# Second layer: the sums of weight blocks on VectorE, ten tiles transposed once and kept in DRAM by columns

## The chip, the core and the metric

The kernel runs on 1 core of a Trainium2 chip. The metric is the device time of one execution in microseconds (us), and a kernel's time is the median of its runs. A core has TensorE (PE in the profile; its weight loads are listed apart as PEld), VectorE (DVE), ScalarE (ACT), GpSimd (POOL) and SyncE (SP), which here only issues transfers. Each engine works through a queue of its own in order, and a wait at the head of a queue holds what is behind it.

## The reference, cut to what matters

Attention over pooled keys gives x, 2304 rows of 512. A first layer sends each row to one of eight experts. The second layer, which the change touches, sends every row through all eight:

```python
def _moe2_ref(x, w_gate, w1, w2):          # x 2304x512, w1 8x512x1024, w2 8x1024x512
    logits = x @ w_gate
    P = np.exp(logits - logits.max())
    for _ in range(8):
        P /= P.sum(1, keepdims=True) + 1e-09
        P /= P.sum(0, keepdims=True) + 1e-09
        P *= N / E
    out = np.zeros((N, D))
    for e in range(E):
        h = np.maximum(x @ w1[e], 0.0)
        out += P[:, e:e + 1] * (h @ w2[e])
```

## The kernel before, in words

Attention and the first layer fill the first 410 us and are not touched. Near the end of that time GpSimd also prepares the weights of expert 0 of the second layer (`ahead`, L947).

**How the second layer is tiled.** The 18 tiles of 128 rows lie in SBUF in `x2`. They are taken in nine pairs, a pair being the two row halves of a two by two block product, and the nine pairs are grouped in five chunks (`CHUNKS`, L1394): tiles 0 to 7 are the "early" four pairs, tiles 8 to 17 the "later" five. Every matrix product of 2x2 blocks is done with seven products in place of eight (the operand sums are formed beforehand, the result sums afterwards). `up` (L1769) makes the hidden values of a pair's half for one expert in seven products of 12 matmuls, `down` (L1870) the output of a pair in seven products of 12 matmuls. Each fp32 operand is split in two fp16 parts, high and low, and three of the four part products are added (`PASSES`). PSUM results are copied, added, passed through ReLU and split again by ScalarE and VectorE (`act`, `tt`, `dve`, `copy`, L1410 to L1449).

**Operands of the rows.** `pair` (L1554) scales two tiles (L1563), transposes them on TensorE (L1572), copies PSUM to SBUF (L1428 or L1430), and forms the seven operand blocks of `xc` by four subtractions `sub` and four splits `cut` (L1416 and L1442). For the early pairs the subtractions run on VectorE for the first pair and on GpSimd for the other three, and for pairs 2 and 3 one of the low splits is on GpSimd too. The ten later tiles are written to DRAM as rows (`xspill`, one transfer of 2560 KB), because half of the weights `w2c` will lie in their place. `build` (L2088) loads them pair by pair and calls `pair` with the subtractions on GpSimd. Before that, `gates_of_rows` (L1637) transposes the same ten tiles a first time (L1654), unscaled, for the gate products (L1661) with `wg2` as the stationary operand of 8 columns; their 8-row results are copied out (L1674) and turned in ten small transposes (L1682). `gates` (L1604, L1619) makes the logits of the early tiles, `balance` (L1692) the eight rounds of normalising.

**Weights of the next expert.** `weights1` (L1483) loads `w1` of the next expert in four transfers of 512 KB (`load_raw`, L1471), forms four sums of blocks for each half k (`sums`, on GpSimd, L1442) and splits seven blocks into fp16 parts (`split`, L1462: high on ScalarE L1418, low on VectorE L1466) into `w1c`. `weights2` (L1517) does the same for `w2` into `w2c`. Both use the one buffer `raw2` and the temporaries `tt[0]`, `tt[1]`, so `w1` of the next expert is loaded when `weights2` has read the buffer, and `w2` when `weights1` has. The last sum of a half is written over a block that was split before.

**What sets the order.** Nothing runs as it is written: each operation is added to a `Plan` (L1019) with its engine, an estimated duration, the names it reads and writes, and a rank, which is its place in the text plus `late`. `run` (L1069) goes through simulated time: a free engine takes, of the tasks whose inputs are finished by then, the one with the lowest rank. What comes out is the fixed order of each queue. The estimates are

```python
def dve_cost(n):
    return n / 960 + 0.068
def pool_cost(n):
    return n / 475 + 0.15
    DMA_WAIT = 2.0        # us after a transfer's bytes
    DMA_RATE = 360e3      # bytes per us, transfers one after the other
```

and 1.285 for a product of 12 matmuls. They know nothing of two engines that slow each other. `run` of `Layer2` (L1975) puts in the early pairs, the first `up`, `gates_of_rows`, the loads of five blocks of `w2c`, `gates`, `balance`, `build`, and then `up` and `down` in turns, with `weights1` behind the last `up` and `weights2` behind the last `down` of an expert (L2044).

Of the kernel before, what the change touches and what calls it, by code (L numbers as in the profile page):

```python
# [20 lines left out]
P = 128  # L21
# [1362 lines left out]
class Chunk:  # L1384
# [11 lines left out]
    Chunk(1, 12, 2, 2),  # L1396
]


class Layer2:  # L1400
# [81 lines left out]

    def weights1(self, e):  # L1483

        g = self.g
        self.load_raw(g.w1b[e], 1)
        raw, s1, s2 = g.raw2, g.tt[0], g.tt[1]

        def q(i, j, k):

            return raw[:, 2 * j + k, i * 512:(i + 1) * 512], ("raw", 2 * j + k, i)

        for k in range(2):
            a11, a21, a12, a22 = q(0, 0, k), q(1, 0, k), q(0, 1, k), q(1, 1, k)
            t1, t2 = (s1[:, k], ("tt", 0, k)), (s2[:, k], ("tt", 1, k))
# [12 lines left out]
            to(3, t1)  # L1508
            to(4, t2)
            to(1, a12)  # L1510
            sums(a21, a11, a21, ALU.subtract)
            to(5, a21)
            to(2, a22)
            sums(a12, a12, t2, ALU.subtract)
            to(6, a12)

    def weights2(self, e):  # L1517
# [5 lines left out]
        for k in range(2):  # L1523

            b11, b12, b21, b22 = [
                (v[:, 2 * j + k, :, l * 256:(l + 1) * 256], ("raw", 2 * j + k, l))
                for j in range(2) for l in range(2)
            ]
            t1, t2 = (s1[:, k], ("tt", 0, k)), (s2[:, k], ("tt", 1, k))

            def sums(o, x, y, op):
                self.tt("gpsimd", o[0], x[0], y[0], op, [x[1], y[1]], [o[1]])

            def to(i, x):
# [12 lines left out]
            to(5, b12)  # L1547
            sums(b21, b21, t2, ALU.subtract)
            to(6, b21)
            to(2, b22)  # L1550

    def pair(self, ch, u, slot, rows, place, eng, low, late=0):  # L1554

        g, nc = self.g, self.nc
        ja, jb = ch.tiles(u)
        (x, xk), (y, yk) = rows, place
        yk = [k if isinstance(k, list) else [k] for k in yk]
        yy = yk[0] + yk[1]  # L1560
        for i, j in enumerate((ja, jb)):
            def scale(i=i, j=j):
                nc.vector.tensor_scalar(  # L1563
                    x[:, i], x[:, i], g.s2[:, j:j + 1], None, op0=ALU.mult
                )

            self.dve(0.34, scale, ["s2"], [xk[i]], late)
            pt, pk = self.bank(f"p{i}")

            def turn(i=i, pt=pt):  # L1570
                for k in range(KC):
                    nc.tensor.transpose(  # L1572
                        pt[:, k * P:(k + 1) * P], x[:, i, k * P:(k + 1) * P], g.ident
                    )

            self.pe(0.5, turn, [xk[i]], [pk], late)
            self.copy(y[:, i], pt, [pk], yk[i], late)
        h = y.rearrange("p i (j n) -> p i j n", j=2)
        xc = g.xc[:, slot]

        def cut(ops, sl, v, reads, who="vector"):
            vv = v.rearrange("p o (k n) -> p o k n", n=P)
# [3 lines left out]
            self.tt(  # L1586
                who, lo, vv, hi, ALU.subtract, list(reads) + [k + (0,) for k in keys],
                [k + (1,) for k in keys], late,
# [47 lines left out]

    def gates_of_rows(self):  # L1637

        g, nc = self.g, self.nc
        rest = NT - SPLIT  # L1640
        cols = g.hs[:, 4].rearrange("p o x f n -> p (o x f n)").bitcast(F32)
        flat = [
            (g.temps["y"][i], [("temp", "y", i, x) for x in range(2)]) for i in range(2)
        ] + [(g.temps["z"][0], [("temp", "z", 0)])]
        for j in range(rest):
            pt, pk = self.bank(("da", "db")[j % 2])
            pl, lk = self.bank("dc")
# [4 lines left out]
            def turn(j=j, pt=pt):  # L1652
                for k in range(KC):
                    nc.tensor.transpose(  # L1654
                        pt[:, k * P:(k + 1) * P], g.x2[:, SPLIT + j, k * P:(k + 1) * P],
                        g.ident,
                    )

            def gate(j=j, pl=pl, col=col):
# [6 lines left out]
            self.pe(0.5, turn, [("x2", SPLIT + j)], [pk])  # L1666
            self.copy(col, pt, [pk], ck)
            self.pe(0.9, gate, ck, [lk])
            if j % 4 == 3 or j == rest - 1:
                n = (j % 4 + 1) * P  # L1670
                f, fk = flat[j // 4]

                def take(n=n, f=f, pl=pl):
                    nc.vector.tensor_copy(f[0:E, 0:n], pl[0:E, 0:n])  # L1674

                self.dve(0.6, take, [lk], fk)
        pt, pk = self.bank("p0")
        po = pt[:, 0:rest * E].rearrange("p (t e) -> p t e", e=E)

        def turn():  # L1680
            for j in range(rest):
                nc.tensor.transpose(  # L1682
                    po[:, j], flat[j // 4][0][0:E, (j % 4) * P:(j % 4 + 1) * P],
                    g.ident[0:E, 0:E],
                )

        self.pe(1.1, turn, [k for _, fk in flat for k in fk], [pk])
        self.dve(
            0.2, lambda: nc.vector.tensor_copy(g.lg2[:, SPLIT:, :], po), [pk], [("lg", 9)]
        )  # L1690

# [77 lines left out]
    def up(self, ch, part, e):  # L1769
# [16 lines left out]
        def product(x, pq, first):  # L1786
# [83 lines left out]
    def down(self, ch, u, e):  # L1870
# [16 lines left out]
        def product(x, pq, first):  # L1887
# [14 lines left out]
            reads += [("w2c", r, k, x) for k in range(2) for x in range(2)]  # L1902
            self.pe(1.285, fn, reads, [t[x][1]])

# [70 lines left out]
    def run(self):  # L1975
# [23 lines left out]
        for i in range(7):  # L1999
            if i not in g.w2x:  # L2000
                w2(i)

        self.dma(
            g.xspill.rearrange("p t n -> p (t n)"),
            g.x2[:, SPLIT:, :].rearrange("p t n -> p (t n)"),
            [("x2", j) for j in range(SPLIT, NT)], ["xspill"],
        )

        other = g.hs[:, 5].rearrange("p o x f n -> p (o x f n)")[:, 0:2048].bitcast(F32)
# [18 lines left out]
        for i, (ch, u) in enumerate(early):  # L2028
            ja, jb = ch.tiles(u)
            ks = [("out", (ja + a * (jb - ja)) // 2, (ja + a * (jb - ja)) % 2) for a in range(2)]  # L2030
            rows = (g.x2[:, ja:jb + 1:jb - ja], ks)
# [56 lines left out]
    def build(self, ch, u, place):  # L2088
# [227 lines left out]
```

## Time and profile before

| | before |
|---|---|
| median of 3 runs (lowest to highest) | 1844.81 us (1841.62 to 1847.65) |
| the profiled execution, its own time | 1842.31 us |
| its span from first to last instruction | 1840.5 us |
| PE busy | 1722.2 us, 94% |
| DVE busy | 1287.6 us, 70% |
| ACT busy | 1024.4 us, 56% |
| POOL busy | 509.2 us, 28% |
| mean granted TensorE clock | 0.979 of full speed |

In a row of instructions the first number is the start in us from the span's start, the second the duration; in square brackets stand the idle time of the engine just before and what ended it. An instruction's duration overlaps the next one's by a little where they run back to back, so the distance between two starts is the time that one takes up.

### The profile page before, as it was taken

How to read it: one execution, taken by the hardware profiler on the slowest of the kernel's cores; microseconds unless marked ns; L12 is line 12 of the kernel's file. 1: busy time of each engine (PE TensorE's matmuls, PEld its weight loads, DVE VectorE, ACT ScalarE, POOL GpSimd, SP SyncE). 2: the span in 40 equal slices, each digit the busy share in tenths (PEclk: the TensorE clock that was granted, in tenths of full speed). 3: DMA queues.
4: the chain of work that ended last, by engine and by line, in shares of the span. 5: the costliest groups of instructions: out<-in, count | busy, mean ns of one | idle time of the engine just before them, and what ended most of it. 6: DMA issues, size and time to landing. Idle time of an engine off the chain costs nothing. (4 is left out here: it accounts for less than half of the span.)

```text
span 1840.5 us, 40536 instructions
## 1 busy us (share of the span) xinstructions
PE 1722.2 (94%) x17273; PEld 1485.3 (81%) x17273; DVE 1287.6 (70%) x2121; ACT 1024.4 (56%) x1880; POOL 509.2 (28%) x446
## 2 busy tenths in 40 slices
PE   6878988888999999999999999999999999999997
PEld 5756766666888879888888888798879888888986
DVE  7876567766887785786678658765875786588564
ACT  4632221335577665765566556656655765576542
POOL 7824688205031220132032103300330132031101
PEclk9988999998999999999999999999999999999999
DMA  9525334449031242234124222422332233133311
GB/s 306 142 59 184 133 123 154 159 141 355 14 116 69 84 135 36 47 96 112 24 71 119 64 35 69 120 66 36 105 115 36 55 96 104 24 80 110 110 47 46
DMA packets 80851, 183.89 MB, mean 100 GB/s; under 512 B 25472, under 2 KB 34688, under 8 KB 78720
## 3 DMA queue, kind: packets, MB, share of 16 engines
q1 hardware_dynamic: 66592, 131.66, 21.4%
q0 software_dynamic: 14048, 49.29, 12.6%
q8 instruction: 148, 2.42, 0.5%
q14 instruction: 63, 0.52, 0.1%
HBM read 121.16 MB, written 59.77 MB: 98 GB/s over the span
## 5 line engine op out<-in xcount | busy, mean ns | idle before, releaser
L1894 PEld LDWEIGHTS <-hs 128*128 128x128 f16 x6048 | 591.5, 98 | 102.2 <-issue 31.8
L1795 PEld LDWEIGHTS <-w1c 128*128 128x128 f16 x6720 | 604.9, 98 | 79.7 <-issue 15.1
L1795 PE MATMUL ua<-xc,w1c 128*128 128x256 f16 (+1 forms) x3840 | 428.4, 263 | 6.6 <-ACT u L1416 5.8
L1894 PE MATMUL da<-x,hs 128*128 128x256 f16 x2592 | 318.3, 273 | 9.3 <-ACT z L1416 7.5
L1795 PE MATMUL uc<-xc,w1c 128*128 128x256 f16 (+1 forms) x1920 | 215.1, 264 | 5.4 <-DVE u L1815 4.4
L1957 POOL DMA_DIRECT2D sums<-x x54 | 46.2, 856 | 612.8 <-ACT x L1418 584.5
L1815 DVE TENSOR_TENSOR u<-u,uc 128x512 f32<-128x512 f32 x144 | 98.5, 684 | 85.3 <-ACT u L1416 70.7
L1815 DVE TENSOR_TENSOR p<-p,ub 128x512 f32<-128x512 f32 x72 | 49.2, 683 | 149.0 <-PE ub L1795 149.0
L1442 DVE TENSOR_TENSOR hs<-u,hs 128x512 f16<-128x512 f32 x144 | 111.3, 773 | 52.4 <-ACT hs L1416 52.4
L1442 DVE TENSOR_TENSOR hs<-h,hs 128x512 f16<-128x512 f32 x144 | 111.2, 773 | 43.0 <-ACT hs L1416 43.0
L1416 ACT COPY u<-ua 128x512 f32<-128x512 f32 x144 | 83.7, 581 | 90.8 <-PE ua L1795 90.3
L1894 PE MATMUL dc<-x,hs 128*128 128x256 f16 x864 | 108.6, 277 | 16.7 <-DVE z L1911 16.7
L1418 ACT ACTIVATE u<-u 128x512 f32<-128x512 f32 x144 | 90.8, 631 | 55.9 <-DVE u L1815 55.9
L1416 ACT CAST hs<-p 128x512 f16<-128x512 f32 x144 | 89.2, 619 | 44.7 <-DVE p L1442 44.7
L841 ACT ACTIVATE wa<-ph 128x512 f32<-128x512 f32 x42 | 25.1, 597 | 148.6 <-issue 70.0
L1442 DVE TENSOR_TENSOR hs<-p,hs 128x512 f16<-128x512 f32 x144 | 106.1, 737 | 2.0 <-ACT hs L1416 2.0
L1894 PE MATMUL da<-w2r,hs 128*128 128x256 f16 x864 | 107.3, 275 | 0.0
L1795 PE MATMUL ub<-xc,w1c 128*128 128x256 f16 (+1 forms) x960 | 106.4, 262 | 0.0
L1894 PE MATMUL dc<-w2r,hs 128*128 128x256 f16 x864 | 106.1, 273 | 0.0
L1894 PE MATMUL db<-x,hs 128*128 128x256 f16 x864 | 106.1, 273 | 0.0
L851 PEld LDWEIGHTS <-wa 128*128 128x128 f16 x504 | 46.9, 98 | 70.1 <-DVE wa L843 12.2
L1442 POOL TENSOR_TENSOR raw<-raw,tt 128x512 f32<-128x512 f32 x28 | 42.1, 1503 | 199.0 <-DVE x L1466 145.7
(287 smaller groups left out, 2819.3 us busy)
## 6 DMA issues: line engine op xcount, KB each, us to landing
raw<-in_moe_w_dram SPq DMA_DIRECT2D x56, 512.0 KB, 4.3
wr<-in_moe_w_dram SPq DMA_DIRECT2D x54, 512.0 KB, 4.4
sums<-x POOLq DMA_DIRECT2D x54, 512.0 KB, 5.1
xc<-cspill SPq DMA_DIRECT2D x14, 1792.0 KB, 7.3
cspill<-xc SPq DMA_DIRECT2D x8, 896.0 KB, 7.0
sums<-x SPq DMA_DIRECT2D x9, 512.0 KB, 3.0
x<-sums SPq DMA_DIRECT2D x9, 512.0 KB, 3.5
wa<-in_k_dram SPq DMA_DIRECT2D x4, 1024.0 KB, 10.7
```

The lines of the kernel that those rows point to most:

```text
L841: nc.scalar.activation(hr[:, sl], ph, AF.Relu, scale=HSC)
L851: nc.tensor.matmul(py, hs[:, a, k, :], w.w2[:, b, k, :], start=(k == 0 and t == 0), stop=(k == FC - 1 and t == 2),)
L1416: self.nc.scalar.copy(o, x)
L1418: self.nc.scalar.activation(o, x, func, scale=scale)
L1442: lambda: e.tensor_tensor(o, x, y, op=op), reads, writes, late,
L1795: nc.tensor.matmul(o, g.w1c[:, l, a, k, f * P:(f + 1) * P], g.xc[:, pr, r, b, k, :], start=(first and fi == 0 and n == 0), stop=(n == 5), ...
L1815: lambda: nc_.tensor_tensor(o_[0], o_[0], x_[0], op=ALU.add),
L1894: nc.tensor.matmul(t[x][0][:, lo], g.hs[:, sl[f // 2], l, a, f % 2, :], g.w2c[r][:, b, f, :], start=(first and n == 0), stop=(n == 11), sk ...
L1957: lambda: nc.gpsimd.dma_start(sums, x, accum_op=ALU.add), xk, [sk],
```

## The change

Four things are edited, all in the second layer.

- **Weight sums.** All sums of `weights1` and `weights2` go from GpSimd to VectorE. Three of the four sums of each half of `weights1`, and the loads in front of them, become `sums1`, put into the plan behind the third `down` of the expert before, with 60 added to their rank; the fourth stays between the splits.
- **Row operands.** All subtractions and low splits of `pair` (now `columns` and `operands`) go to VectorE; early pairs 2 and 3 get 60 added to their rank.
- **Later tiles.** `later_columns` scales each of the ten tiles, transposes it once, copies it to one of three buffers, makes its gate product with the tile as the stationary operand and the 8 columns of `wg2` moving, straight into one PSUM bank, and writes the buffer to DRAM (ten transfers of 256 KB). The small transposes and the copies before them go. `build` loads the tile already scaled and transposed.
- **Estimate.** A product counts 1.305 in the plan in place of 1.285.

The diff, cut to its core:

```diff
--- before.py
+++ after.py
+PAIRS = [(ch, u) for ch in CHUNKS for u in range(ch.nt)]
...
-    def weights1(self, e):
+    def blocks1(self, k):
+        raw, s1, s2 = self.g.raw2, self.g.tt[0], self.g.tt[1]
+        a11, a21, a12, a22 = [
+            (raw[:, 2 * j + k, i * 512:(i + 1) * 512], ("raw", 2 * j + k, i))
+            for j in range(2) for i in range(2)
+        ]
+        return a11, a12, a21, a22, (s1[:, k], ("tt", 0, k)), (s2[:, k], ("tt", 1, k))
+
+    def sums(self, o, x, y, op, late=0):
+        self.tt("vector", o[0], x[0], y[0], op, [x[1], y[1]], [o[1]], late)
+
+    def sums1(self, e):
+        late = 60
+        self.load_raw(self.g.w1b[e], 1)
+        for k in range(2):
+            a11, a12, a21, a22, t1, t2 = self.blocks1(k)
+            self.sums(t1, a21, a22, ALU.add, late)
+            self.sums(t2, t1, a11, ALU.subtract, late)
+            self.sums(a21, a11, a21, ALU.subtract, late)
+
+    def weights1(self):
...
-        self.load_raw(g.w1b[e], 1)
...
-            def sums(o, x, y, op):
-                self.tt("gpsimd", o[0], x[0], y[0], op, [x[1], y[1]], [o[1]])
...
-            sums(t1, a21, a22, ALU.add)
-            sums(t2, t1, a11, ALU.subtract)
             to(0, a11)
             to(3, t1)
             to(4, t2)
             to(1, a12)
-            sums(a21, a11, a21, ALU.subtract)
             to(5, a21)
             to(2, a22)
-            sums(a12, a12, t2, ALU.subtract)
+            self.sums(a12, a12, t2, ALU.subtract)
             to(6, a12)

     def weights2(self, e):
...
-            def sums(o, x, y, op):
-                self.tt("gpsimd", o[0], x[0], y[0], op, [x[1], y[1]], [o[1]])
+            sums = self.sums
...
-    def pair(self, ch, u, slot, rows, place, eng, low, late=0):
+    def columns(self, x, xk, j, y, yk, bank, late=0):
+        g, nc = self.g, self.nc
+        self.dve(
+            0.4, lambda: nc.vector.tensor_scalar(x, x, g.s2[:, j:j + 1], None, op0=ALU.mult),
+            ["s2"], [xk], late,
+        )
+        pt, pk = self.bank(bank)
+        def turn():
+            for k in range(KC):
+                nc.tensor.transpose(
+                    pt[:, k * P:(k + 1) * P], x[:, k * P:(k + 1) * P], g.ident
+                )
+        self.pe(0.5, turn, [xk], [pk], late)
+        self.copy(y, pt, [pk], yk, late)
+
+    def operands(self, slot, place, late=0):
...
         def sub(o, a, b):
-            self.tt(eng, o, a, b, ALU.subtract, yy, yy, late)
+            self.tt("vector", o, a, b, ALU.subtract, yy, yy, late)
...
-        cut((3, 5), slice(3, 6, 2), h[:, :, 0], yy, low)
+        cut((3, 5), slice(3, 6, 2), h[:, :, 0], yy)
...
-    def gates_of_rows(self):
+    def later_columns(self):
...
+        pl, lk = self.bank("dc")
         for j in range(rest):
...
+            self.columns(
+                g.x2[:, SPLIT + j], ("x2", SPLIT + j), SPLIT + j, col, ck, ("da", "db")[j % 2]
+            )
+            def gate(j=j, col=col):
                 for k in range(KC):
                     nc.tensor.matmul(
-                        pl[0:E, (j % 4) * P:(j % 4 + 1) * P], g.wg2[:, k, :],
-                        col[:, k * P:(k + 1) * P], start=(k == 0), stop=(k == KC - 1),
+                        pl[:, j * E:(j + 1) * E], col[:, k * P:(k + 1) * P], g.wg2[:, k, :],
+                        start=(j == 0 and k == 0), stop=(k == KC - 1),
+                        skip_group_check=(j > 0),
                     )
...
+            self.pe(0.5, gate, ck, [lk])
+            self.dma(g.xspill[:, j], col, ck, [("xspill", j)])
+        def scale():
+            nc.vector.tensor_tensor(
+                g.lg2[:, SPLIT:, :], pl[:, 0:rest * E].rearrange("p (t e) -> p t e", e=E),
+                g.inv2[:, SPLIT:].unsqueeze(2).to_broadcast([P, rest, E]), op=ALU.mult,
+            )
+        self.dve(0.2, scale, [lk, "s2"], [("lg", 9)])
...
-            self.pe(1.285, fn, reads, [t[x][1]])
+            self.pe(1.305, fn, reads, [t[x][1]])
...
-        self.dma(
-            g.xspill.rearrange("p t n -> p (t n)"),
-            g.x2[:, SPLIT:, :].rearrange("p t n -> p (t n)"),
-            [("x2", j) for j in range(SPLIT, NT)], ["xspill"],
-        )
...
-            eng, low = [("vector",) * 2, ("gpsimd", "vector"), ("gpsimd",) * 2][min(i, 2)]
-            self.pair(ch, u, i, rows, (places[0], other, places[2], places[1])[i], eng, low)
+            place = (places[0], other, places[2], places[1])[i]
+            late = 0 if i < 2 else 60
+            for a, j in enumerate((ja, jb)):
...
+                self.columns(
+                    g.x2[:, j], ("out", j // 2, j % 2), j, place[0][:, a], ks, f"p{a}", late
+                )
+            self.operands(i, place, late)
             self.keep(ch, u)
...
-                (self.weights1 if kind == "u" else self.weights2)(e + 1)
+                if kind == "u":
+                    self.weights1()
+                else:
+                    self.weights2(e + 1)
+            if kind == "d" and e + 1 < E and i % len(PAIRS) == 2:
+                self.sums1(e + 1)

         one("u", 0)
-        self.gates_of_rows()
+        self.later_columns()
...
-            self.dma(place[0][:, k], g.xspill[:, j - SPLIT], ["xspill"], [place[1][k]], late)
-        self.pair(ch, u, ch.pair + u, place, place, "gpsimd", "vector", late)
+            self.dma(
+                place[0][:, k], g.xspill[:, j - SPLIT], [("xspill", j - SPLIT)], [place[1][k]],
+                late,
+            )
+        self.operands(ch.pair + u, place, late)
```

## Rows read from the trace of the kernel before

**Rows 1.** The page: busy time, share of the span, instructions of each engine.

```profile
PE 1722.2 (94%) x17273; PEld 1485.3 (81%) x17273; DVE 1287.6 (70%) x2121; ACT 1024.4 (56%) x1880; POOL 509.2 (28%) x446
```

**Rows 2.** Busy time by stretch: us, engines with instructions, PE clock, DMA share, GB/s.

```profile
840.00:860.00 20.00, 17.04 (x141) 14.40 (x140) 12.37 (x19) 10.07 (x19) 4.13 (x3) 0.91 0.29 65
...
941.00:1021.00 80.00, 74.79 (x678) 66.01 (x676) 67.67 (x94) 53.41 (x106) 32.09 (x20) 1.00 0.38 103
1021.00:1101.00 80.00, 80.00 (x818) 72.63 (x816) 43.38 (x72) 47.01 (x88) 4.26 (x5) 1.00 0.27 57
```

**Rows 3.** What PE waited for, 590 to 1815 us: us in total, times, longest.

```profile
PE dc L1894 <- DVE z L1911: 16.7, 6, 3.0
PE da L1894 <- ACT z L1416: 6.6, 12, 1.6
PE uc L1795 <- DVE u L1815: 4.4, 5, 0.9
PE ua L1795 <- ACT u L1416: 4.1, 7, 3.0
PE da L1894 <- ACT y L1416: 1.3, 6, 0.2
```

**Rows 4.** Timeline of POOL, DVE and PE, 1008 to 1019 us.

```profile
1009.79 1.71 POOL L1442 TENSOR_TENSOR raw<-raw 128x512 f32<-128x512 f32 x1
...
1010.41 1.65 DVE L1442 TENSOR_TENSOR u<-p,u 128x512 f32<-128x512 f32 x1
...
1017.00 0.41 DVE L1911 TENSOR_TENSOR z<-z,dc 128x256 f32<-128x256 f32 x1
...
1017.46 1.47 PE L1894 MATMUL dc<-x,hs 128*128 128x256 f16 x12 [2.96 <-DVE z L1911]
```

**Rows 5.** Timeline of DVE, 1121 to 1125 us, no POOL instruction beside it.

```profile
1123.11 0.68 DVE L1442 TENSOR_TENSOR hs<-h,hs 128x512 f16<-128x512 f32 x1
1123.71 0.68 DVE L1466 SCALAR_TENSOR_TENSOR w1c<-raw,w1c 128x512 f16<-128x512 f32 x1
```

**Rows 6.** Waits of the whole span: POOL for loads of weight blocks.

```profile
POOL tt L1442 <- DMA raw<-in_moe_w_dram: 71.2, 22, 5.3
```

**Rows 7.** Transfers that touch raw, 997 to 1020 us.

```profile
DMA to landing us min/median/max: 4.4/5.1/6.4
```

**Rows 8.** Timeline of PE, 427 to 461 us.

```profile
427.65 0.60 PE L1654 MATMUL da<-ident,x 128*128 128x128 f32 x4
428.08 1.11 PE L1572 MATMUL pt<-ident,x 128*128 128x128 f32 x8
...
429.56 1.04 PE L1661 MATMUL dc<-hs,wg 128*8 128x128 f32 x8
430.53 1.09 PE L1572 MATMUL pt<-ident,x 128*128 128x128 f32 x8
...
457.64 0.66 PE L1682 MATMUL pt<-ident,y 8*128 8x8 f32 x8
459.38 0.38 PE L1682 MATMUL pt<-ident,z 8*128 8x8 f32 x2 [1.09 <-DVE z L1674]
```

**Rows 9.** Timeline of PE's weight loads, 456 to 480 us.

```profile
456.70 0.91 PEld L1619 LDWEIGHTS <-xc 128*128 128x128 f16 x30
...
478.89 0.30 PEld L1745 LDWEIGHTS pt<-prob,ones 128*128 128x128 f32 x2
```

**Rows 10.** Busy time by stretch, start of the second layer.

```profile
420.00:440.00 20.00, 18.42 (x138) 14.79 (x139) 14.55 (x26) 13.52 (x28) 8.07 (x8) 0.87 0.98 372
440.00:460.00 20.00, 18.68 (x189) 15.48 (x187) 15.20 (x19) 11.25 (x21) 15.08 (x13) 0.98 1.02 416
460.00:480.00 20.00, 19.15 (x222) 16.41 (x222) 14.20 (x35) 11.43 (x22) 0.00 (x0) 0.84 0.08 33
```

**Rows 11.** Line 1442: a subtraction of half width on DVE, min/median/max ns.

```profile
L1442 DVE TENSOR_TENSOR tt<-tt x4: 413/417/942, 428.0 to 433.8; 128x256 f32<-128x256 f32 x4
```

**Rows 12.** DMA issues of the page: size and us to landing.

```profile
rows<-xspill SPq DMA_DIRECT2D x4, 256.0 KB, 6.9
```

More of the change, by code (lines that the diff above doesn't have):

```diff
@@ L1481, in load_raw @@
             self.dma(o, x, [], keys, late)
-    def weights1(self, e):
+    def blocks1(self, k):
[16 more added lines that the diff above has]
+    def weights1(self):
         g = self.g
-        self.load_raw(g.w1b[e], 1)
-        raw, s1, s2 = g.raw2, g.tt[0], g.tt[1]
-        def q(i, j, k):
-            return raw[:, 2 * j + k, i * 512:(i + 1) * 512], ("raw", 2 * j + k, i)
         for k in range(2):
-            a11, a21, a12, a22 = q(0, 0, k), q(1, 0, k), q(0, 1, k), q(1, 1, k)
-            t1, t2 = (s1[:, k], ("tt", 0, k)), (s2[:, k], ("tt", 1, k))
-            def sums(o, x, y, op):
-                self.tt("gpsimd", o[0], x[0], y[0], op, [x[1], y[1]], [o[1]])
+            a11, a12, a21, a22, t1, t2 = self.blocks1(k)
             def to(i, x):
@@ L1550, in weights2, with cut @@
             to(2, b22)
-    def pair(self, ch, u, slot, rows, place, eng, low, late=0):
+    def columns(self, x, xk, j, y, yk, bank, late=0):
         g, nc = self.g, self.nc
-        ja, jb = ch.tiles(u)
-        (x, xk), (y, yk) = rows, place
+        self.dve(
[11 more added lines that the diff above has]
+    def operands(self, slot, place, late=0):
+        g = self.g
+        y, yk = place
         yk = [k if isinstance(k, list) else [k] for k in yk]
         yy = yk[0] + yk[1]
[L1561 to L1564, printed above, removed]
-                )
[L1567 to L1577, printed above, removed]
         h = y.rearrange("p i (j n) -> p i j n", j=2)
         xc = g.xc[:, slot]
-        def cut(ops, sl, v, reads, who="vector"):
+        def cut(ops, sl, v, reads):
             vv = v.rearrange("p o (k n) -> p o k n", n=P)
@@ L1586, in cut @@
             self.tt(
-                who, lo, vv, hi, ALU.subtract, list(reads) + [k + (0,) for k in keys],
+                "vector", lo, vv, hi, ALU.subtract, list(reads) + [k + (0,) for k in keys],
                 [k + (1,) for k in keys], late,
@@ L1641, in gates_of_rows @@
         cols = g.hs[:, 4].rearrange("p o x f n -> p (o x f n)").bitcast(F32)
-        flat = [
-            (g.temps["y"][i], [("temp", "y", i, x) for x in range(2)]) for i in range(2)
-        ] + [(g.temps["z"][0], [("temp", "z", 0)])]
+        pl, lk = self.bank("dc")
         for j in range(rest):
-            pt, pk = self.bank(("da", "db")[j % 2])
-            pl, lk = self.bank("dc")
             i = j % 3
@@ L1650, in gates_of_rows @@
             ck = [("hs", 4, o, x) for o in (2 * i, 2 * i + 1) for x in range(2)]
[L1652 to L1659, printed above, removed]
+            self.columns(
+                g.x2[:, SPLIT + j], ("x2", SPLIT + j), SPLIT + j, col, ck, ("da", "db")[j % 2]
+            )
@@ L1660, in gate @@
+            def gate(j=j, col=col):
                 for k in range(KC):
                     nc.tensor.matmul(
-                        pl[0:E, (j % 4) * P:(j % 4 + 1) * P], g.wg2[:, k, :],
-                        col[:, k * P:(k + 1) * P], start=(k == 0), stop=(k == KC - 1),
-                    )
[L1666 to L1690, printed above, removed]
+                        pl[:, j * E:(j + 1) * E], col[:, k * P:(k + 1) * P], g.wg2[:, k, :],
@@ L1902, in product @@
             reads += [("w2c", r, k, x) for k in range(2) for x in range(2)]
-            self.pe(1.285, fn, reads, [t[x][1]])
+            self.pe(1.305, fn, reads, [t[x][1]])
         def copy(o, k, x):
@@ L2001, in run @@
                 w2(i)
-        self.dma(
-            g.xspill.rearrange("p t n -> p (t n)"),
-            g.x2[:, SPLIT:, :].rearrange("p t n -> p (t n)"),
-            [("x2", j) for j in range(SPLIT, NT)], ["xspill"],
-        )
         other = g.hs[:, 5].rearrange("p o x f n -> p (o x f n)")[:, 0:2048].bitcast(F32)
@@ L2029, in run @@
             ja, jb = ch.tiles(u)
-            ks = [("out", (ja + a * (jb - ja)) // 2, (ja + a * (jb - ja)) % 2) for a in range(2)]
-            rows = (g.x2[:, ja:jb + 1:jb - ja], ks)
-            eng, low = [("vector",) * 2, ("gpsimd", "vector"), ("gpsimd",) * 2][min(i, 2)]
-            self.pair(ch, u, i, rows, (places[0], other, places[2], places[1])[i], eng, low)
+            place = (places[0], other, places[2], places[1])[i]
+            late = 0 if i < 2 else 60
+            for a, j in enumerate((ja, jb)):
+                ks = place[1][a] if isinstance(place[1][a], list) else [place[1][a]]
+                self.columns(
+                    g.x2[:, j], ("out", j // 2, j % 2), j, place[0][:, a], ks, f"p{a}", late
+                )
+            self.operands(i, place, late)
             self.keep(ch, u)
```

## The prediction

> **What bounds the kernel now.** I began with the busy times of the page: PE is busy 94% of the span, DVE 70%, POOL 28% [rows 1]. So the question is where PE is not busy, and the busy times by stretch answer it. In the 80 us from 1021 PE is busy 80.00 of 80 at the full clock; in the 80 us before, in which both weight blocks of an expert are changed, it is busy 74.79 [rows 2]. The same pair of stretches returns with every expert, seven times. The second layer is therefore bound by PE, except at the changes of weights.
>
> Next, the waits of PE from 590 to 1815 us, which hold all these changes: 16.7 for the add on z, 6.6, 4.4, 4.1 and 1.3 for the copies and adds of ScalarE and VectorE, 33.1 us together, and none for a weight or a transfer [rows 3]. So VectorE is late there, not the weights. The timeline shows why: a subtraction that takes 0.68 us takes 1.65 beside a subtraction of POOL, the add on z that PE needs starts only at 1017.00, and PE stands for 2.96 us [rows 4, 5]. Without POOL beside it VectorE starts one such instruction every 0.60 us [rows 5], which is what the plan's formula gives for 512 elements (0.601). The queues' order was worked out for that pace and is wrong wherever POOL stretches it.
>
> After four of the long waits PE's granted clock is 0.91 over a stretch of 20 us of which one stands in [rows 2], so part of it ran at 1.2 and not 2.4 GHz: 4 x 20 x 0.09 = 7.2 us. All changes of weights together cost 33.1 + 7.2 = 40.3 us.
>
> **The change part by part.**
>
> Weight sums, what they add to VectorE. An expert has 16 sums of 512 elements, 16 x 0.60 = 9.6 us. What goes: from 941 to 1021 VectorE is busy 67.67 us with 94 instructions, in the quiet stretch 43.38 with 72, or 0.603 each [rows 2]; 94 x 0.603 = 56.6, so 11.0 us were stretching. VectorE would be busy 67.67 - 11.0 + 9.6 = 66.3 of 80 us: no more than now, but in pieces of 0.60 that the plan knows. GpSimd keeps its transfers' issues (5 instructions in the quiet 80 us [rows 2]); nothing waits behind the sums on its queue.
>
> What that gives at the changes of weights. The 16.7 us on z go, and 3.0 of the 4.1, the longest wait, and half of the 6.6. Of the other 10.1 (waits of up to 0.9) I let half stay, since the sums and splits still crowd VectorE. That is 23.0 + 5.1 = 28.1, and the clock's 7.2 with it, as no wait near 3 us is left: **-35.3 us**. Ends: -40.3 and, if only the stretch's net 1.4 us per expert is gained, -9.8.
>
> Loads. The sums' waits for weight blocks move from POOL's queue, where they cost nothing, to VectorE's, where the adds for PE stand behind them. POOL waits 71.2 us in 22 waits [rows 6], but counted from when it had nothing else to do. The plan expects a block 512 KB / 360 + 2.0 = 3.46 us after issue; these land after 4.4 to 6.4, median 5.1 [rows 7], 1.6 late. It costs only where VectorE came to the sum at once, which a rank 60 later makes rare for w1; there are 14 sets of loads, seven of each weight. I take **+3 us**; ends 0 and, from 2.9 us at each set, +41.
>
> PE's own work. Ten transposes of four go, 428.08 - 427.65 = 0.43 us each: -4.3. The gate products take 430.53 - 429.56 = 0.97 per tile now [rows 8]. Afterwards 8 instructions each load 128 columns of fp32 for 8 columns of work, which no row shows. Bounds: 0.91 / 30 = 0.030 per load (fp16, 8 columns of work) and 0.30 / 2 = 0.15 (fp32, 144 columns) [rows 9], so 0.24 to 1.2 us per tile, or -7.3 to +2.3 in all. The nearest is an fp32 transpose with a load of 128 columns, 0.43 / 4 = 0.109: 0.87 per tile, -1.0. The Trainium skill (TensorE: Matmul & The Clock Gate, section Weight-path perf modes) says that fast weight load is off when the input is FP32. By that the 0.030 end falls away, and the saving would end at about -6.3 and not at -12.6. The small transposes go as well: 0.66 + 0.38 [rows 8], -1.0. Together **-6.3 us**; ends -12.6 and -3.0.
>
> Start of the layer. From 420 to 480 PE is idle 3.75 us and the missing clock is worth 20 x (0.13 + 0.02 + 0.16) = 6.2 us [rows 10]. The 2.6 of the first stretch follow the idle time before it and stay. The wait of 1.09 for a copied gate result [rows 8] goes with that copy. The first `up` no longer queues behind unscaled tiles' transposes. Against it, VectorE takes over 12 subtractions of half width at 0.41 [rows 11] (4.9 us), two low splits (1.2), six weight sums (3.6) and ten scales, moved here from `build`, at the 0.4 of the diff's estimate (4.0); three copies go (1.8 at 0.60 each). Net 11.9 us into 16 us of idle VectorE [rows 10], less what the POOL instructions there stretch now. If that cover is gone, it costs up to 12. Ten writes with three buffers make a tile's copy wait for the write three tiles before; the nearest row for 256 KB is 6.9 us to landing [rows 12] where the plan counts 2.7, 4.2 late, for 7 / 3 rounds: up to +9.8. SP issues ten transfers for one, idle otherwise, and the five blocks of `w2c` behind them are first needed by `down`. Ends -7.4 and +10; I take **-3 us**.
>
> `build`. Its subtractions (20 x 0.41 = 8.2 us) come to VectorE, ten scales and up to ten copies leave it and ScalarE: even, nothing. The estimate 1.305 moves no work: nothing by itself.
>
> Sum: -35.3 + 3 - 6.3 - 3 = -41.6. The profiled execution took 1842.3, so 1800.7. It lies 2.5 under the median of the runs shown; against that median the forecast is **1803 us**. A measurement of this kernel can tell about 0.3% from no change, some 5.5 us.
>
> **The rivals.**
>
> VectorE's load, not the stretch. VectorE has 66 of 80 us to do either way; if PE's waits follow its load, an expert gains 1.4 us: 7 x 1.4 = 9.8, with a third of the clock (2.4) and the -9.3 of the other parts: -21.5, about 1823. For it: 1.4 us is little. Against: PE's longest waits each end on one add behind stretched instructions [rows 3, 4]. The Trainium skill (Perfetto Trace Analysis, section Optimizing Scalar/DVE Operations) says much the same, that moving work between GpSimd and VectorE might not help as they share a read port; the trace agrees on the sharing [rows 4].
>
> The sums are not ahead. The plan goes by what is ready and by rank, so POOL's sums of w1 already ran as soon as the block had landed, at the change of w2 [rows 4]. If VectorE does its six at that place, 3.6 us stand in front of the add on z where some 5 us of stretching stood (five instructions at 1.05 more). Six times 1.7 is gained, 10 of the 33.1, half the clock (3.6), and the -9.3: about 1822. The rank of 60 later and a busy VectorE speak against it.
>
> VectorE waits for the blocks. All 71.2 us of POOL's waits [rows 6] pass to VectorE and on to PE: -44.6 + 71.2, so +27, about 1871. It decides from 44.6 / 14 = 3.2 us lost per set of loads. Against it: that is the whole landing time after issue less about 2 us, as if VectorE never had other work.
>
> **How the numbers follow.** The forecast has 0.64, VectorE's load 0.22, sums not ahead 0.08, waiting for blocks 0.05, the rest 0.01. The likeliest gives 1803. Low end: 5 more at the changes of weights, 6 in PE's work and 5 at the start: 1787. High end: the two rivals near 1823 with up to 9 us of the start's bound: 1832; the last rival stays outside. Faster by over 0.3%: 0.92, from the first three less a little for their ends; within 0.3%: 0.03; slower: 0.05.
>
> **What the profile afterwards would show.** Right: no 128x512 instruction of VectorE above 0.8 us beside POOL, no PE wait on z near 3 us, no stretch of 20 us at 0.91 after 500 us, DVE's busy time about unchanged, POOL's lower by some 190 us (112 sums at up to 1.71 [rows 4]); at the start L1563's place taken by ten early scales, and fewer transposes from 480 to 560. Wrong: VectorE waiting for raw at length; PE waiting in 420 to 480 on copies that wait for xspill; PE still idle 5 us per expert without stretched instructions; gate products over 1 us per tile.

## The result and the profile after

The changed kernel takes **1797.66 us** (median of 4 runs, 1789.91 to 1798.56) where the kernel before took 1846.23 (4 runs, 1841.62 to 1850.68) beside it: a ratio over the runs of 0.9728, 95% interval 0.9691 to 0.9765 (the two medians alone give 0.9737), or 48.6 us less. In a later series it took 1786.00 us against 1839.35: 0.971 (0.9689 to 0.9731). The profiled execution took 1796.94, its span is 1795.2.

Busy time, share of the span and instructions of each engine, from the page of the changed kernel:

```profile
PE 1706.6 (95%) x17223; PEld 1485.7 (83%) x17223; DVE 1268.6 (71%) x2262; ACT 1022.5 (57%) x1872; POOL 278.6 (16%) x300
```

Against [rows 1], POOL has lost 230.6 us and 146 instructions. VectorE has 141 more instructions and is busy 19 us *less*: the work that came to it is smaller than the stretching that it was freed of. PE is busy 15.6 us less and waits much less. Where, the stretches say (columns as in [rows 2]):

```profile
420.00:440.00 20.00, 9.90 (x63) 8.86 (x64) 12.33 (x31) 8.04 (x16) 0.00 (x0) 0.74 0.65 237
440.00:460.00 20.00, 19.20 (x198) 17.56 (x197) 19.70 (x41) 14.14 (x26) 0.00 (x0) 1.00 0.98 395
460.00:480.00 20.00, 20.00 (x213) 18.18 (x212) 14.13 (x30) 10.64 (x21) 0.00 (x0) 0.74 0.68 232
...
941.00:1021.00 80.00, 80.00 (x802) 72.49 (x800) 59.93 (x102) 53.06 (x102) 4.27 (x5) 1.00 0.44 119
1021.00:1101.00 80.00, 80.00 (x753) 71.90 (x751) 51.57 (x86) 52.74 (x101) 3.39 (x4) 1.00 0.19 34
1101.00:1181.00 80.00, 80.00 (x767) 72.08 (x765) 63.23 (x109) 53.08 (x102) 3.97 (x5) 1.00 0.42 119
```

Three 80-us stretches in a row, longer together than one expert and with both of its changes of weights in them: PE is busy throughout, at the full clock; before, one of two such stretches lost 5.2 us [rows 2]. VectorE is busy 52 to 63 of 80 there. In fact PE waits for nothing at all from 590 to 1770 us: the list of [rows 3], 33.1 us in 36 waits, is empty after the change (in the second profile of the same kernel it has two waits of 0.5).

What VectorE now waits for, from 590 to 1760 us (us in total, times, longest):

```profile
DVE p L1800 <- PE ub L1780: 136.2, 43, 3.6
...
DVE tt L1443 <- DMA raw<-in_moe_w_dram: 1.8, 1, 1.8
```

VectorE is mostly early and waits for PE and ScalarE; it met a weight block that had not landed once, for 1.8 us, where POOL had met 22 for 71.2 us [rows 6].

**Where the time came from.** PE's timeline cut at the same points of the work in both profiles, in us (the start of the product that holds the 504th matmul of the products ends the start of the layer; two matmuls of 128 columns count as one of 256):

| stage | before | after | difference |
|---|---|---|---|
| up to PE's last work of layer 1 | 410.3 | 419.9 | +9.6 |
| gap to PE's first work of layer 2 | 10.2 | 9.2 | -1.0 |
| to the first product | 10.9 | 5.8 | -5.1 |
| to the 504th matmul of the products | 76.8 | 79.8 | +3.0 |
| to the 1008th | 60.9 | 55.5 | -5.4 |
| the rest, with all changes of weights | 1271.4 | 1225.0 | -46.4 |

The first line is no effect of the change: layer 1 is the same code, and in the other twelve profiles (before, and the eleven runs below) it ends between 406.6 and 413.2 us. So this one profile hides some 10 us of what was gained: layer 2 alone went from 1430.2 to 1375.3, by 54.9.

The -46.4 of the last line can be put together from the trace of before: 33.1 us of waits, 7.2 of low clock, and 36 times 0.16 us. A product of 12 matmuls is shown with 1.47 us, but where PE waits for nothing the next one starts 1.31 after it, as the timeline of PE in the changed kernel shows:

```profile
1062.13 1.47 PE L1879 MATMUL db<-x,hs 128*128 128x256 f16 x12
1063.44 1.47 PE L1879 MATMUL da<-x,hs 128*128 128x256 f16 x12
1064.75 1.47 PE L1780 MATMUL ua<-xc,w1c 128*128 128x256 f16 x12
1066.06 1.47 PE L1879 MATMUL da<-x,hs 128*128 128x256 f16 x12
```

Each wait also loses that overlap of 0.16. 33.1 + 7.2 + 5.8 = 46.1.

That the largest of these waits come from stretched instructions can be read from the kernel before. Between 1006.65 and 1017.00, where the add on z starts [rows 4], VectorE does not pause, and beside POOL's six sums it shows

```profile
1007.24 1.46 DVE L1442 TENSOR_TENSOR hs<-h,hs 128x512 f16<-128x512 f32 x1
1008.62 1.75 DVE L1442 TENSOR_TENSOR s<-u,u 128x512 f32<-128x512 f32 x1
...
1011.98 1.75 DVE L1442 TENSOR_TENSOR hs<-s,hs 128x512 f16<-128x512 f32 x1
...
1013.98 1.42 DVE L1442 TENSOR_TENSOR p<-s,p 128x512 f32<-128x512 f32 x1
1015.33 1.75 DVE L1442 TENSOR_TENSOR hs<-u,hs 128x512 f16<-128x512 f32 x1
```

With the one of [rows 4] these are six instructions that take 5.6 us more than at 0.69 each, and PE waits 2.96 for the add behind them. The same holds for each of the six waits on z: six stretched instructions in an unbroken run of nine, 5.3 to 5.6 us too long together, and a wait of 1.9 to 3.0 us.

### The profile page after: what moved, and what is told of

Its sections match the earlier page's. It is cut to its first block, busy times and chain, and to the rows that moved or that the text cites. A ratio compares the mean times of both kernels' runs of the same rounds, so it can differ in the third digit from the quotient of the medians.

```text
span 1795.2 us, 40336 instructions
## 1 busy us (share of the span) xinstructions
PE 1706.6 (95%) x17223; PEld 1485.7 (83%) x17223; DVE 1268.6 (71%) x2262; ACT 1022.5 (57%) x1872; POOL 278.6 (16%) x300
## 5 line engine op out<-in xcount | busy, mean ns | idle before, releaser
L1443 DVE TENSOR_TENSOR hs<-h,hs 128x512 f16<-128x512 f32 x144 | 98.8, 686 | 43.2 <-ACT hs L1417 43.2
L1443 DVE TENSOR_TENSOR hs<-u,hs 128x512 f16<-128x512 f32 x144 | 98.7, 686 | 39.3 <-ACT hs L1417 39.3
L851 PEld LDWEIGHTS <-wa 128*128 128x128 f16 x504 | 47.1, 99 | 69.6 <-DVE wa L843 10.2
L1443 DVE TENSOR_TENSOR hs<-p,hs 128x512 f16<-128x512 f32 x144 | 98.3, 683 | 0.6 <-ACT hs L1417 0.6
L1419 ACT ACTIVATE p<-p 128x512 f32<-128x512 f32 x72 | 45.2, 628 | 86.2 <-DVE p L1800 86.2
```

Source lines behind the costliest of these rows:

```text
L851: nc.tensor.matmul(py, hs[:, a, k, :], w.w2[:, b, k, :], start=(k == 0 and t == 0), stop=(k == FC - 1 and t == 2),)
L1419: self.nc.scalar.activation(o, x, func, scale=scale)
L1443: lambda: e.tensor_tensor(o, x, y, op=op), reads, writes, late,
```

## The experiments

The theory: POOL's sums stretch VectorE's instructions, the order of the queues was worked out for unstretched ones, and it breaks where they are stretched. The rivals: it is VectorE's total load; it is the placing of the sums half an expert ahead; the rest of the change does the work. No kernel here leaves out part of the computation; three of them add work. The expected times were reckoned from 1798, the first measurement. In the three series below the kernel before takes 1839.35 to 1840.53 and the queues of the change take 1786 to 1787, so what counts is the difference within a series.

**The sums on VectorE, and nothing else of the change** (in the kernel before, both `weights1` and `weights2`):

```
-                self.tt("gpsimd", o[0], x[0], y[0], op, [x[1], y[1]], [o[1]])
+                self.tt("vector", o[0], x[0], y[0], op, [x[1], y[1]], [o[1]])
```

> The kernel before with one word changed in weights1 and weights2: all sums on VectorE, in their old places. Stretching (VectorE's instructions grow beside POOL's, and the queues' order no longer fits): the waits of PE after 590 us fall from 33.1 us to under 3, and with them go the 7.2 us of low clock and the overlap lost at each wait, about 46 us in all: 1846 - 46 = 1800 us. VectorE's load (PE's waits follow the busy time of VectorE, which changes by 1.4 us per expert): about 1836 us, with 23 us of waits left. The place of the sums half an expert ahead carries the gain: no gain here, 1846 us.

Measured: 1797.47 us against 1839.99, 0.9772 (0.975 to 0.9794). One word in two places gives 42.5 us, some 80% of the 53.1 that the queues of the change gain in the same series (1786.94, under "Not ahead"). What PE still waited for, 590 to 1770 us:

```profile
PE da L1894 <- ACT z L1416: 2.5, 5, 0.6
PE da L1894 <- ACT y L1416: 2.0, 3, 0.9
```

4.5 us in 8 waits stay (under 3 had been expected), all of them on ScalarE's copies and none on an add of VectorE.

**The whole change, but the sums on POOL**:

```
     def sums(self, o, x, y, op, late=0):
-        self.tt("vector", o[0], x[0], y[0], op, [x[1], y[1]], [o[1]], late)
+        self.tt("gpsimd", o[0], x[0], y[0], op, [x[1], y[1]], [o[1]], late)
```

> The changed kernel with the sums of both weights back on POOL, everything else of the change kept (places, row operands on VectorE, tiles transposed once, estimate). Stretching: the waits after 590 us come back, 25 to 40 us, and only the start keeps its gain of some 9 us: about 1837 us. VectorE's load: VectorE has 9.6 us per expert less to do by itself and PE waits little: about 1805 us. The place carries the gain: about 1800 us.

Measured: 1848.37 us, 1.0058 (1.0035 to 1.0081) against before: everything is lost, and a little more (with the start's gain kept, some 9 us less than before had been expected). PE's waits, 590 to 1815 us:

```profile
PE dc L1879 <- DVE z L1896: 22.5, 13, 3.0
PE ua L1780 <- ACT u L1417: 12.9, 13, 1.6
PE da L1879 <- ACT z L1417: 6.0, 6, 1.8
PE uc L1780 <- DVE u L1800: 4.6, 6, 0.8
PE da L1879 <- ACT y L1417: 1.1, 1, 1.1
```

47.1 us in 39 waits, the same names as [rows 3]. The add on z is late 13 times where it was 6 before. Why more than before was not separated: the sums' place, the edits of rows and the estimate all differ from the kernel before. Nor does all that POOL's sums cost have to run through VectorE. ScalarE splits the sums, and from 590 to 1770 us it waited for those of POOL 4.3 us in 7 waits before and 12.0 in 6 here; how much of that reached PE was not separated either.

**POOL reads beside VectorE.** The sums stay on VectorE with all queues as in the change; POOL only does, into a tile that nobody reads, one more operation with two inputs behind each sum:

```
+        def both():
+            fn()
+            self.nc.gpsimd.tensor_tensor(by, o[0], o[0], op=op)
```

> The changed kernel, and behind each of the 112 sums on VectorE POOL does one more operation of two SBUF inputs and 512 elements, on the sum's result and into a spare buffer that nobody reads. The order of all other queues stays what it is. Stretching: VectorE's instructions beside these take up to 1.77 us again and 20 to 45 us of waits and low clock come back: 1818 to 1843 us. VectorE's load: VectorE's work is the same, so 1798 us, within 5.

Measured: 1811.15 us, 0.9842 (0.9818 to 0.9866): 24.2 us above the queues of the change in the same series (1786.94). VectorE's and PE's work is that of the change and POOL's results are used by nobody; neither VectorE nor ScalarE waits for POOL; still 19.4 us of PE's waits come back between 590 and 1770 us, in 29 waits, the largest two groups:

```profile
PE ua L1789 <- ACT u L1417: 9.8, 19, 0.9
PE da L1888 <- ACT y L1417: 8.6, 7, 1.4
```

and VectorE's instructions of one shape are stretched (min/median/max in ns, first and last start in us):

```profile
L1443 DVE TENSOR_TENSOR hs<-p,hs x144: 676/685/1521, 433.3 to 1780.0; 128x512 f16<-128x512 f32 x144
...
L1443 DVE TENSOR_TENSOR raw<-raw x28: 673/1103/1526, 467.2 to 1626.7; 128x512 f32<-128x512 f32 x28
...
L1443 DVE TENSOR_TENSOR tt<-raw,tt x14: 925/1522/1525, 607.2 to 1625.2; 128x512 f32<-128x512 f32 x14
```

In the timeline of this kernel the first sums of an expert show the pair side by side:

```profile
606.22 4.26 POOL L1501 TENSOR_TENSOR by<-tt 128x512 f32<-128x512 f32 x3
...
608.05 1.52 DVE L1443 TENSOR_TENSOR raw<-raw 128x512 f32<-128x512 f32 x1
...
610.23 1.47 PE L1789 MATMUL uc<-xc,w1c 128*128 128x256 f16 x12 [0.28 <-DVE u L1809]
```

The last stage of the table grew from 1225.0 to 1250.2, by 25.2; 19.4 of waits and 29 x 0.16 of lost overlap are 24.0. That is about half of the 46.4 that the sums on POOL had cost, and the waits on z are hardly among it (0.3 us): the bystander's instructions follow VectorE's sums one by one and stand elsewhere than the six sums in a row of the kernel before. So the run shows that stretching alone costs PE time; that it made the add on z late is read from the rows of the kernel before, above.

**POOL is busy beside VectorE, but writes.** At the same place POOL copies one column of the sum, which keeps its place behind it, and then fills its tile three times:

```
+            self.nc.gpsimd.tensor_copy(by[:, 0:1], some)
+            for _ in range(3):
+                self.nc.gpsimd.memset(by, 0.0)
```

> The changed kernel, and behind each of the 112 sums on VectorE POOL copies one column of the result and then fills a spare buffer of 512 elements three times, so that it is busy as long as one of its old sums but reads next to nothing from SBUF. If it is the reading of SBUF by POOL that stretches VectorE: VectorE's instructions stay near 0.68 us and the time at 1798 us, within 6. If any work of POOL does it: 1818 to 1843 us.

Measured: 1786.69 us against 1840.53, 0.9697 (0.967 to 0.9725): no loss, though POOL is now busier than before the change (page, and line 1443 of the same kernel):

```profile
PE 1703.0 (95%) x17223; PEld 1483.5 (83%) x17223; DVE 1266.3 (71%) x2262; ACT 1021.7 (57%) x1872; POOL 520.3 (29%) x748
...
L1443 DVE TENSOR_TENSOR hs<-p,hs x144: 673/685/693, 434.9 to 1755.6; 128x512 f16<-128x512 f32 x144
...
L1443 DVE TENSOR_TENSOR raw<-raw x28: 672/685/689, 468.2 to 1602.3; 128x512 f32<-128x512 f32 x28
...
L1443 DVE TENSOR_TENSOR tt<-raw,tt x14: 684/685/694, 607.5 to 1601.7; 128x512 f32<-128x512 f32 x14
```

Where POOL reads 128x512, the same instructions take up to 1521 to 1526 ns; where it writes, 689 to 694. So it is not that POOL is busy, but that it reads; a POOL instruction with one full-size input was not tried. The Trainium skill (SBUF — State Buffer, section Who interferes with whom) says that a VectorE instruction with two inputs in SBUF contends with a GpSimd instruction that reads SBUF and not with one that only writes it. The trace agrees, with 1.52 against 0.69 us.

**More load on VectorE.** The first two of the four sums of each half are done three times, in `sums1` and likewise in `weights2`, 112 more instructions in all:

```
+            for _ in range(3):
+                self.sums(t1, a21, a22, ALU.add, late)
+                self.sums(t2, t1, a11, ALU.subtract, late)
```

> The changed kernel with the first two sums of each half formed three times over (the repeats give the same values): 16 sums of 512 elements more per expert on VectorE, 9.6 us of busy time, known to the planner. Stretching: the order still fits, so little of it reaches PE: 1798 to 1810 us. VectorE's load: 7 x 9.6 = 67 us more on VectorE, of which PE sees most: 1840 to 1865 us.

Measured: 1786.83 us, 0.9703 (0.9679 to 0.9727), no loss against the change. VectorE is busy 1329.1 us (74%) in it, more than in the kernel before, and PE waits once, for 0.5 us, from 590 to 1770. The first rival falls.

**Not ahead.** The rank of 60 and the place half an expert earlier are undone:

```
-        late = 60
+        late = 0
...
                 if kind == "u":
+                    self.sums1(e + 1)
                     self.weights1()
...
-            if kind == "d" and e + 1 < E and i % len(PAIRS) == 2:
-                self.sums1(e + 1)
```

> The changed kernel with sums1 not ahead: the loads and the three sums per half stand at the head of weights1 again, with nothing added to their rank. The planner puts out the same queues, instruction by instruction, so this is also a second look at the changed kernel. Stretching: 1798 us, within 4. The place carries the gain: slower, by up to 25 us. The part of the span ahead of the second layer, which was 9.6 us longer in the profile of the changed kernel though its code is the same: if that is chance, it will end between 410 and 420 us here and in the other runs, with no regard to the kernel.

Measured: 1786.94 us, 0.9721 (0.9698 to 0.9744). The planner makes the same queues of it: in the second layer the instructions of every engine are those of the changed kernel in the same order, and only line numbers differ. The half expert in the change's description is no part of its effect, since the plan takes a sum when its block is there and VectorE is free, wherever the source calls for it.

**The estimate of a product.** The change had raised it from 1.285 to 1.305; here it is put back in both places, for `up` and for `down`:

```
-            self.pe(1.305, fn, reads, [t[x][1]])
+            self.pe(1.285, fn, reads, [t[x][1]])
```

> The changed kernel with the plan's estimate of a product back at 1.285. The estimate moves no work, it only changes which task is taken when; a product takes 1.31 us. Theory: no more than 5 us from 1798 either way. Rival: with the lower estimate PE's order runs ahead of VectorE's, and up to 15 us of waits come back.

Measured: 1791.87 us (1788.39 to 1794.77), 0.9737 (0.9712 to 0.9762). That is 5.0 and 5.2 above the two kernels of the same series whose estimate is 1.305 (1786.83 and 1786.69), though the intervals overlap. The waits of PE, 590 to 1770 us, are like those that the first experiment had left:

```profile
PE da L1879 <- ACT z L1417: 2.9, 6, 0.6
PE da L1879 <- ACT y L1417: 1.5, 3, 0.8
```

The stage after the 1008th matmul takes 1230.3 us, 5.3 more than in the changed kernel, and 4.4 + 9 x 0.16 = 5.8. The other order that follows from 1.285 also has a gain in its profile: from the end of layer 1 to the 1008th matmul it takes 146.5, where the change takes 150.3, with the clock at 1.00 from 460 to 480 us (see "The gates spread"). So the layer as a whole takes 1376.8 in this profile, 1.5 more than in the change.

**The sums and the estimate alone** (the first experiment, with 1.285 turned to 1.305):

> The kernel before with the sums on VectorE and the estimate of a product at 1.305, and nothing else of the change. With the estimate at 1.285 some 4.5 us of waits were left at the changes of weights. If the estimate accounts for those: no waits after 590 us and 5 us less than with the sums alone, about 1792 us on that chip. If the work on the rows accounts for them: 1797 us.

Measured: 1788.79 us against 1839.35, 0.9717 (0.9697 to 0.9737). The last stage takes 1224.6 us, as in the changed kernel, and PE waits once, for 0.5 us, from 590 to 1770. In the same series the changed kernel was run again:

> The changed kernel itself once more, beside the two below on one chip. By the run with the same queues (1786.9 us there, 0.972 of the kernel before): 0.972 again, within 0.003.

1786.00 us, 0.971 (0.9689 to 0.9731). So the words "vector" and 1.305 alone give 50.6 of 53.4 us. What is left for all the edits of rows (transposed once, scaled early, kept by columns, subtractions on VectorE, gates turned) is 2.8 us, and the intervals do not tell it from nothing. The profiles, with layer 1 left out, say much the same: from the end of layer 1 to the end of the span 1377.2 us here, 1375.3 and 1374.6 in the two profiles of the change. The edits were not tried one by one.

**The gates spread.** Why the edits of rows give so little is in the start of the layer. In the changed kernel, and in its second profile, PE's clock is low from 460 to 480 us though PE is busy without a break there: 0.74 above, and 0.83 in the second profile. There the timeline of the changed kernel shows:

```profile
464.26 0.96 PE L1660 MATMUL dc<-wg,hs 128*128 128x8 f32 x8
465.07 0.63 PE L1572 MATMUL db<-ident,x 128*128 128x128 f32 x4
465.54 0.90 PE L1626 MATMUL pt<-wg2h,xc 128*128 128x8 f16 x30
466.30 1.04 PE L1660 MATMUL dc<-wg,hs 128*128 128x8 f32 x8
467.19 0.63 PE L1572 MATMUL da<-ident,x 128*128 128x128 f32 x4
467.66 0.90 PE L1626 MATMUL pt<-wg2h,xc 128*128 128x8 f16 x30
468.42 1.66 PE L1660 MATMUL dc<-wg,hs 128*128 128x8 f32 x8
...
470.81 1.71 PE L1660 MATMUL dc<-wg,hs 128*128 128x8 f32 x8
...
473.18 2.72 PE L1780 MATMUL ua<-xc,w1c 128*128 128x256 f16 x12
475.69 2.77 PE L1780 MATMUL uc<-xc,w1c 128*128 128x256 f16 x12
...
479.37 0.81 PE L1780 MATMUL ua<-xc,w1c 128*128 128x256 f16 x6
```

Gates with 8 columns and transposes follow each other with no product between them, then the same gate takes 1.66 and 1.71 instead of 0.96 us, and products take 2.72 and 2.77 instead of 1.47: PE runs at 1.2 GHz, the lower of its two levels. So the gates' fp16 products were given later ranks:

```
         self.pe(
-            0.9, products, [("xc", slot, o, x) for o in range(4) for x in range(2)], [pk]
+            0.9, products, [("xc", slot, o, x) for o in range(4) for x in range(2)], [pk],
+            (50, 55, 70, 85)[slot],
         )
```

> The changed kernel with the ranks of the four gate products of the early tiles raised by 50, 55, 70 and 85, so that the short matmuls of 8 columns no longer stand in one run from 465 to 473 us but one by one between products of 12 matmuls. In the changed kernel's profile the granted clock falls to 0.74 over the stretch from 460 to 480 us though PE waits for nothing; 20 x 0.26 = 5.2 us. If the run of short matmuls brings the clock down: clock near 1.00 in that stretch and 3 to 5 us less, about 1793 us. If the clock falls for another reason, no change; if the later logits hold up the balance and with it the first outputs, up to 10 us more.

> The changed kernel with the gate products of the early tiles spread, a second time, to tell its 4 us from the spread of the runs. Clock: 3 to 5 us under the changed kernel on the same chip. Chance: no difference beyond 2 us.

Measured: 1782.71 us (1782.05 to 1787.78), 0.9694 (0.9671 to 0.9717), which is 4.0 and 4.1 under the kernels with POOL's fills and with more load in its series, and in the series with the changed kernel 1784.58 (1780.43 to 1785.91), 0.9688 (0.9669 to 0.9707). The clock in this kernel's second profile (columns as above):

```profile
440.00:460.00 20.00, 20.00 (x210) 18.75 (x208) 19.70 (x39) 15.76 (x30) 0.00 (x0) 1.00 0.85 301
460.00:480.00 20.00, 20.00 (x256) 18.54 (x254) 18.85 (x38) 12.54 (x24) 0.00 (x0) 1.00 0.52 166
```

The low clock of this stretch is gone in both profiles, and the stage from the first product to the 504th matmul takes 74.8 and 74.5 us, where the changed kernel has 79.8 and 78.1. The estimate at 1.285 gives a third order of the start, in which products stand between the gates as well; there too the clock is 1.00 from 460 to 480 us, while in all six profiles whose PE goes through the start in the order of the change it is 0.74 to 0.83. The time moves in the same direction, by 1.4 us beside the changed kernel: within the spread of either. Part of that spread is layer 1. Without it, from its end to the end of the span, the three profiles with the queues of the change (the change twice, not ahead) take 1374.6 to 1375.3 us and the two with the gates spread 1370.0 and 1372.0. By its profiles it is thus the best version of the study, by 2.6 to 5.3 us, but by its times it can't be told from the change.

## Why the prediction was right, and where its steps were off

The forecast was 1803 us in 1787 to 1832, by the mechanism of the stretched instructions. The sign and the range hold, and the gain was larger than the sum's 41.6 us: 48.6 in the first runs, 53.4 in the later series.

- **Changes of weights, -35.3, ends to -40.3.** Mechanism right: the rows of the kernel before show the add on z late behind stretched instructions, and the two runs with a bystander on POOL that the stretching costs PE time. Size: -46.4 in the last stage, beyond the far end. Two things are missing in the sum. The first is the step that failed: **"the estimate 1.305 moves no work: nothing by itself"**. In the last stage it measured 5.8 us (1230.4 to 1224.6 between the two kernels with the sums and nothing else of the change), and 5.3 back again (1225.0 to 1230.3 in the change with 1.285). The sum let half of the 10.1 us of short waits stay, 5.05; with the sums alone 4.5 did stay. But they stood on the estimate: a product takes 1.31 of PE's time, a plan that counts 1.285 is some 2% short on each, and with the other order that follows from 1.305 these waits are gone as well. What in the two orders makes the copies late or not was not followed up. The second is that a wait was counted by its recorded length and not by the 0.16 us of overlap that it also loses: 36 x 0.16 = 5.8.
- **Loads, +3.** Nothing: VectorE waited once, for 1.8 us, and PE not at all. The term was too careful; the bound of +41 was far away.
- **VectorE's load.** Forecast 66.3 of 80 us at a change; the two stretches show 59.9 and 63.2. As forecast, the sums cost VectorE no more than the stretching had: 1268.6 us busy after, 1287.6 before.
- **PE's own work -6.3 and start -3.** Together -9.3. From the end of layer 1 to the 1008th matmul the change goes from 158.8 to 150.3, so -8.5, but the sums and the estimate alone take 152.6 there (9.6 + 10.1 + 73.0 + 59.9), -6.2 without any of the edits that the two terms were made of. Of these, 3.6 are the clock from 440 to 480, at 0.98 and 0.84 before and at 1.00 with the sums and the estimate alone. That the total fits is therefore luck in good part. Single parts came as forecast: a tile's gate takes 0.82 us (0.87 forecast, 0.97 before), since the timeline of the changed kernel has one at 438.32 and the product behind it at 439.14, and the first product starts 5.1 us sooner. Then 20 x 0.26 = 5.2 us go back to the low clock from 460 to 480. The bounds of the start did not have it: the sum took from the rows that the clock falls after PE stood idle, and here it fell while PE worked.
- **The 7.2 us of clock** went as forecast: from 500 to 1780 us every stretch of 20 us has 1.00. So did POOL's time: some 190 us forecast for the sums, and 195.4 gone with the sums alone (509.2 to 313.8 us); the change's 230.6 hold the row operands too. PE nowhere waited for the columns kept in DRAM.
- **Rivals.** VectorE's load as the bound (0.22) is refuted by the run with 112 more sums, and VectorE waiting for blocks (0.05) by the trace of after. Sums not ahead (0.08) had its place right and its price wrong. In the changed kernel VectorE does the six sums of w1 right behind the change of w2, as POOL did: in one expert from 988.55 to 997.45 us, with one of the six in front of the add on z at 991.89 and not all, and PE waits for nothing. Where the source places them does not matter: both placings give one set of queues and one time. The Trainium skill (Perfetto Trace Analysis, section Optimizing Scalar/DVE Operations) says that moving work between GpSimd and VectorE might not help. Here the move alone gave 2.3% (0.9772): VectorE's instructions at 1.65 us had stood in an order worked out for 0.60.

Still open: which of the edits of rows gains or loses; why the change with its sums on POOL is slower than before; how much of the sums' cost on POOL is ScalarE's waiting for them; and what exactly in the sequence of the start makes PE's clock fall.

## What to carry to other kernels

Where an order is worked out ahead from durations, ask first which instructions take longer than the plan counts beside others, and take what stretches them away from beside them; the moved work may even cost its new engine less than the stretching did. An estimate that is 2% short on the instruction that the plan repeats most is a term of its own, so price it by the short waits of the bound engine. And price a wait of PE at its recorded length plus the overlap of the instruction before it.

## What the runs showed of the hardware that was not expected

- **VectorE beside POOL.** A 128x512 instruction of VectorE with two inputs takes 0.68 us alone, up to 1.53 beside a POOL sum of that size in the run with a bystander and 1.77 in the kernel before, and at most 0.69 beside POOL instructions that only fill a tile of that size. In this kernel POOL could thus stay busy beside VectorE, as long as it only wrote.
- **PE's clock under short matmuls.** The granted clock over 20 us was 0.74 and 0.83 in two profiles of the changed kernel while PE was busy for 20.00 of 20.00 us, behind gates with 8 columns that followed each other; with products between the gates it was 1.00 in three profiles. The busy column shows nothing of this, so the clock column has to be read beside it.
- **A spread that is not the kernel's.** Layer 1, the same code in all kernels here, ended at 406.6 to 413.2 us in twelve profiles and at 419.9 in the thirteenth. A comparison of two profiles stage by stage shows such a difference; a comparison of two spans would have put it down to the change.
